# Sliding-window attention and an ELU layer on one core: the first layer's minimum made by two ScalarE activations in 56 of 144 slots, and two steps of the Strassen-Winograd tiles moved

## The chip, the cores and the metric

The kernel runs on one core of a Trainium2 chip. The core has five engines that each take their own instructions in order: TensorE (PE, with its weight loads as PEld), VectorE (DVE), ScalarE (ACT), GpSimd (POOL) and SyncE (SP), which here only issues transfers. The metric is the device time of one execution in microseconds (us), as the median of several executions. A profile of one execution goes with it.

## The reference, cut to what matters

```python
# attention: batch 8, heads 8, sequence 576, head size 64, window 128
scores = where(0 <= rel < 128, q @ k.T / 8 - slope[h] * |rel|, -1e9)
x = softmax(scores) @ v                      # reshaped to 4608 tokens x 512
# two layers, w_in 512 x 2048, w_out 2048 x 512
h = x @ w_in
g = where(h > 0, h, exp(minimum(h, 0)) - 1)  # ELU
out = g @ w_out                              # 4608 x 512, float32
```

The change touches `g` and `out`. The kernel writes the ELU as max(h, min(exp(h), 1) - 1), which is the same function; exp(minimum(h, 0)) is the same number as min(exp(h), 1).

## The kernel before, in words

The 4608 tokens are nine blocks of 512 (`NTB`). The program is written out in **slots**, numbered from 0. Each slot has at most one `hidden` step: a piece of the first layer that fills one PSUM bank with 128 x 512 numbers (two groups of 128 hidden features for 256 tokens in the later blocks, four for 128 tokens in the early ones). There are 144 such steps, one for each of slots 0 to 17 and 24 to 149. Two banks, `hp[0]` and `hp[1]`, take turns, so the `hidden` step of slot s can't start before the step of slot s-2 has been read out of its bank.

Reading out a bank takes three engines in a row. ScalarE writes e = exp(h) from the bank into SBUF (L305). GpSimd makes the minimum with 1, in place (L306). VectorE then writes g = max(e - 1, h) as float16 (`elu`, L313), reading h from the bank again, which sets the bank free. `elu` of slot s-1 is put into VectorE's queue in slot s, straight after the `hidden` step of slot s.

The main loop at the end (L646 to L659) sets the order inside a slot: the slot's early tasks (ScalarE's softmax exponentials), the `hidden` step, `elu` of the slot before, the slot's tasks (in the order in which they were registered: attention first, the sums of the second layer after that), the output matmuls, and the late tasks. As every engine takes its queue in order, that order decides who stands behind whom.

Attention for batches 2 to 7 is woven in between. A unit of 128 keys takes four slots, say from slot a: late in slot a PE makes the scores into four banks; at the head of slots a+1 and a+2 ScalarE makes two exponentials each (L231); in a+1 and a+2 VectorE multiplies them with a table (`weigh`, L236), the half for heads 0 to 3 first; in slot a+3 PE multiplies with the values (L266), heads 0 to 3 first, and VectorE divides (L271, L272). The units start at slots 32, 36, 40, 44, then 49, 53, 57, 61, then 66 and so on up to 129; after about slot 133 there is no attention left.

The second layer is done in tiles of 256 tokens, n = 0 to 17. Ten of them are plain matmuls (`output`). The eight of `SEVEN` = 5, 7, 9, 11, 13, 15, 16, 17 use the Strassen-Winograd scheme, seven block products in place of eight. For them VectorE makes four sums of blocks of g (`sums`, S1 to S4, L358 through L343) and PE makes `product` 1 to 7 with the sums and with combinations of the weights that `quarters` made beforehand in slots 41 to 48. With s = 15 + 8n, products 1, 6, 2, 7, 5, 4, 3 of tile n are spread over slots s to s+7, seven matmuls in each slot. S1 is made in slots s-2 and s-1, S2 (which reads S1) in s-1, S3 in s+1, S4 in s+3. Product 6 reads S2 and starts as the second matmul of slot s+1. The products stand in two banks, `op` and `av`, 256 columns each (`places`): 1 and 2 in one half bank, 6 and 7 in another, 5 and 3 in a third, 4 in the fourth. Product 2 adds onto product 1 in its half bank, 7 onto 6, 3 onto 5. So product 1 is copied out by ScalarE (L390, tile U1) before product 2 starts, and product 5 likewise (tile U5). VectorE's `combine` makes U2 and U3 from them and the four quarters of the result: C11 is a ScalarE copy (L392), C12, C21 and C22 are additions. C22 = U3 + U5, both in SBUF, stands among the tasks of slot s+6 (of s+8 for n = 16); C21 comes late in slot s+6, C12 late in s+7. The second half of the tile's rows is stored when both C21 and C22 are there. Tile 17, the last, has an order of its own in slots 148 to 153.

Of the kernel before, what the change touches and what calls it, by code (L numbers as in the profile page):

```python
# [10 lines left out]
AF = mybir.ActivationFunctionType  # L11
# [7 lines left out]
def kernel(  # L19
# [9 lines left out]
    nc = tc.nc  # L29
    B, H, S, D = q.shape  # L30
    NTOK, DO = out.shape
    FF = moe_w_in.shape[1]
    NFC = FF // 128
    NTB = NTOK // 512
# [114 lines left out]
    with tc.manual_schedule():  # L149
# [139 lines left out]

        es, gs, hps = {}, {}, {}  # L290

        def hidden(t, c0, w, f0, nf, p):
            hps[t, c0, f0] = p
            a = (512 * t + c0) % RING
            cuts = [(0, w, a)] if a + w <= RING else [(0, RING - a, a), (RING - a, w, 0)]
            for l in range(nf):
                fc = f0 + l
                for u0, u1, x0 in cuts:
                    for c in range(4):
                        nc.tensor.matmul(  # L300
                            p[:, l * w + u0:l * w + u1], w_in_sb[:, c, fc * 128:(fc + 1) * 128],
                            xT[:, c, x0:x0 + u1 - u0], start=(c == 0), stop=(c == 3))
            e = es[t, c0, f0] = work.tile([128, 512], F32, name="e", tag="e", bufs=6)
            n = w * nf
            nc.scalar.activation(e[:, 0:n], p[:, 0:n], AF.Exp)  # L305
            nc.gpsimd.tensor_scalar(out=e[:, 0:n], in0=e[:, 0:n], scalar1=1.0, scalar2=0.0,  # L306
                                    op0=ALU.min, op1=ALU.max)
# [30 lines left out]
        def A(n, i, k):  # L338
            c = 256 * (n % 2) + 128 * i
            return gs[n // 2][:, 8 * k:8 * k + 8, c:c + 128]  # L340

        def add(o, a, b, op=ALU.add):
            V.tensor_tensor(out=o, in0=a, in1=b, op=op)  # L343
# [6 lines left out]
        SS, U, obs = {}, {}, {}  # L350
# [9 lines left out]
        def places(n):  # L360


            x, y = (op, av) if n - 1 in SEVEN else (av, op)
            return ((x, 0), (y, 0), (x, 256), (y, 256)) if n < 2 * NTB - 1 else (
                (sp[2], 0), (sp[3], 0), (sp[0], 0), (hp[0], 0))

        def place(n, i):
            o, c = places(n)[(0, 0, 2, 3, 2, 1, 1)[i - 1]]
            return o[:, c:c + 256]

        def kept(n, i):
            if (n, i) not in U:
                U[n, i] = work.tile([128, 256], F32, name=f"U{i}", tag=f"U{i}", bufs=1)
            return U[n, i]

        def tile_out(n, i):
            if (n, i) not in obs:
                obs[n, i] = work.tile([128, DO], F32, name="ob", tag="ob")
            return obs[n, i]

        def product(n, i, j0=0, j1=8, o=None, c0=0, c1=256):
            a, b = {1: lambda: (A(n, 0, 0), WB(0, 0)), 2: lambda: (A(n, 0, 1), WB(1, 0)), 3: lambda: (SS[n, 4], WB(1, 1)),
                    4: lambda: (A(n, 1, 1), T[4]), 5: lambda: (SS[n, 1], T[1]), 6: lambda: (SS[n, 2], T[2]),
                    7: lambda: (SS[n, 3], T[3])}[i]()
            o = place(n, i) if o is None else o
            for j in range(j0, j1):
                nc.tensor.matmul(o[:, 0:c1 - c0], a[:, j, :], b[:, j, c0:c1], start=j == 0 and i in (1, 4, 5, 6),  # L387
                                 stop=j == 7, skip_group_check=True)
            if j1 == 8 and i in (1, 5):
                nc.scalar.copy(kept(n, i), o)  # L390
            if j1 == 8 and i == 2:
                nc.scalar.copy(tile_out(n, 0)[:, 0:256], o)  # L392

        def combine(n, what):
            if what == "U2":
                add(kept(n, 2), kept(n, 1), place(n, 6))
            elif what == "U3":
                add(kept(n, 3), kept(n, 1), place(n, 7))
            elif what == "C22":
                add(tile_out(n, 1)[:, 256:512], kept(n, 3), kept(n, 5))  # L400
            elif what == "C12":
                add(tile_out(n, 0)[:, 256:512], kept(n, 2), place(n, 3))
                put(n, 0, 0, DO)
            else:
                add(tile_out(n, 1)[:, 0:256], kept(n, 3), place(n, 4))
            if what in ("C22", "C21") and n < 2 * NTB - 1:
                if (n, "half") in U:
                    put(n, 1, 0, DO)
                U[n, "half"] = True

        def put(n, i, c0, c1):
            r = 256 * n + 128 * i
            nc.sync.dma_start(out[r:r + 128, c0:c1], tile_out(n, i)[:, c0:c1])

        def last_piece(n, o, c0, c1, e):
            product(n, 4, 0, 8, o, c0, c1)
            add(tile_out(n, 1)[:, c0:c1], kept(n, 3)[:, c0:c1], o[:, 0:c1 - c0])
            put(n, 1, c0, e)
# [74 lines left out]
        def at(s, f, *a):  # L493
            tasks.setdefault(s, []).append((f, a))

        def after(s, f, *a):
            late.setdefault(s, []).append((f, a))
# [14 lines left out]
        for t in range(2, NTB):  # L512
            for j in range(16):
                step = (128 * (j // 4), 128, 4 * (j % 4), 4) if t < 4 else (256 * (j // 8), 256, 2 * (j % 8), 2)
                HID[16 * t + 6 + j] = [(t, *step, BUF[(j + 1) % 2])]
        SEVEN = (17, 5, 7, 9, 11, 13, 15, 16)
        for o in range(16 * NTB):
            t, ts, f = o // 16, o // 4 % 4, o % 4
            if o // 8 in SEVEN:
                continue  # L520
            s = (9, 11, 13, 14)[o] if o < 4 else 11 + o if o < 13 else 2 * o - 1 if o < 16 else 15 + o
            OUT[s] = [(output, (t, ts, 4 * f, (op, op, sp[3], op)[ts] if t == 0 else (op, av)[ts % 2]))]

        def done(r):
            for step in HID[r]:
                elu(*step)
# [65 lines left out]
        for b in range(2, B):  # L592
# [14 lines left out]
            for n in range(4):  # L607
                piece = (b, int(n < 2), n % 2)
                if b == 2:
                    m = 4 if n < 2 else 6  # L610
# [13 lines left out]
        for n in SEVEN:  # L624
            s = 15 + 8 * n
            if n < 2 * NTB - 1:
                m = 6 if n >= 8 else 4
                for d, i, j in ((-2, 1, (0, m)), (-1, 1, (m, 8)), (-1, 2, ()), (1, 3, ()), (3, 4, ())):
                    at(s + d, sums, n, i, *j)
                at(s + (6 if n + 2 < 2 * NTB else 8), combine, n, "C22")  # L630
                for d, what in ((2, "U2"), (4, "U3"), (6, "C21"), (7, "C12")):
                    after(s + d, combine, n, what)
                for d in range(8):
                    OUT[s + d] = [(product, (n, i, j, j + 1)) for i, j in turns[7 * d:7 * d + 7]]
            else:
                at(s - 3, sums, n, 3)
                for i in (1, 2):
                    at(s - 2, sums, n, i, 0, 6)
                    at(s - 1, sums, n, i, 6, 8)
                at(s - 1, product, n, 1)  # L640
                OUT[s] = [(product, (n, 2)), (product, (n, 6)), (combine, (n, "U2")), (sums, (n, 4))]
                OUT[s + 1] = [(product, (n, 5)), (product, (n, 7)), (combine, (n, "U3"))]
                OUT[s + 2] = [(product, (n, 3)), (combine, (n, "C12")), (combine, (n, "C22")),
                              (last_piece, (n, hp[0], 128, 256, DO)), (last_piece, (n, hp[1], 0, 128, 128))]

        slots = set(HID) | set(OUT) | set(tasks) | set(early)  # L646
        for s in range(min(slots), max(slots) + 1):
            for f, a in early.get(s, []):
                f(*a)
            for step in HID.get(s, []):  # L650
                hidden(*step)
            if s - 1 in HID and s not in (1, 4, 5):
                done(s - 1)
            for f, a in tasks.get(s, []):
                f(*a)
            for f, a in OUT.get(s, []):
                f(*a)
            for f, a in late.get(s, []):
                f(*a)  # L659
# [30 lines left out]
```

## Time and profile before

| what | value |
|---|---|
| median of 8 executions | 318.13 us (317.83 to 319.32) |
| the profiled execution's own time | 317.95 us |
| its span, first to last instruction | 316.2 us |
| busy PE, PEld, DVE, ACT, POOL | 307.3, 237.7, 242.6, 178.2, 175.3 us |
| granted TensorE clock over the span | 1.000 |

The page's busy times are sums over the span; a matmul's listed end is modelled, and lies later than the moment at which the next one may start: the eight matmuls of a 256-column `hidden` step start 0.11 us apart and the step is listed with 1.03 us. Real waiting of PE is therefore read from the distance between two starts, less the work between them, and a wait that the profile lists is shorter than that by up to 0.17 us. In the lists of groups, a row gives the line, the engine, the operation, the tile written and those read, the shape, the count, and then busy us and the mean ns of one, and the idle time before them with what ended it. In the timeline a row gives the start, the duration, and then the same names, with idle time and its end in brackets.

### The profile page before, as it was taken

The page shows a single profiled execution, that of the slowest core. Times are in us where ns is not written, and L with a number is a line of the kernel's source. Part 1 is how long each engine was busy: PE and PEld are TensorE (multiplying, and loading weights), DVE is VectorE, ACT ScalarE, POOL GpSimd, SP SyncE. Part 2 cuts the span into 40 slices and gives each one's busy share as a digit, 9 for nine tenths or more (in the row PEclk, how much of TensorE's full clock was granted, in tenths as well). Part 3 has the DMA queues.
Part 4 walks back from the last instruction along what each step waited for, and adds up shares of the span by engine and source line. Part 5 has one row for each costly group of instructions (what it writes and reads, how often), then busy time and mean ns, then how long its engine had stood idle before and what let it go on. Part 6 is the DMA issues. An engine that isn't in the chain of part 4 may idle for free.

```text
span 316.2 us, 9800 instructions
## 1 busy us (share of the span) xinstructions
PE 307.3 (97%) x4119; PEld 237.7 (75%) x4119; DVE 242.6 (77%) x458; ACT 178.2 (56%) x327; POOL 175.3 (55%) x263
## 2 busy tenths in 40 slices
PE   8999999999999999999999999999999999999995
PEld 6788874887767778876887678767877787778784
DVE  5647566786689888986997798779987787576774
ACT  5575558656666466546665566556644665544330
POOL 8947878573756455664756476645623333334330
PEclk9999999999999999999999999999999999999999
DMA  9999999994979779693969699994932112120103
GB/s 100 177 198 202 202 176 162 142 122 70 100 94 111 98 84 97 76 159 62 112 69 160 98 97 64 153 127 68 75 85 55 38 21 85 52 58 2 66 2 133
DMA packets 96363, 32.02 MB, mean 101 GB/s; under 512 B 83904, under 2 KB 91840, under 8 KB 96320
## 3 DMA queue, kind: packets, MB, share of 16 engines
q0 software_dynamic: 75920, 18.36, 62.0%
q1 hardware_dynamic: 20400, 13.05, 16.5%
q8 instruction: 32, 0.52, 0.7%
q14 instruction: 11, 0.09, 0.1%
HBM read 36.70 MB, written 9.44 MB: 146 GB/s over the span
## 4 chain that ended last, share of the span: by engine, by line
PE 78%; DVE 14%; issue 3%; ACT 3%; POOL 1%; DVEq 0%; ACTq 0%
PE hp L300 32%; PE op L319 11%; PE av L319 6%; PE av L387 5%; DVE g L313 5%; PE op L387 5%; PE spa L225 4%; PE spa L266 3%; DVE S L343 2%; DVE EX L236 2%; ACT EX L231 2%; PE op L424 2%; POOL e L306 1%; DVE s L343 1%; PE sp L248 1%
## 5 line engine op out<-in xcount | busy, mean ns | idle before, releaser
L306 POOL TENSOR_SCALAR e<-e 128x512 f32<-128x512 f32 x144 | 95.8, 666 | 128.4 <-ACT e L305 127.5
L300 PE MATMUL hp<-xT,wi 128*128 128x128 f16 (+2 forms) x1744 | 144.9, 233 | 3.4 <-DVE g L313 2.9
L300 PEld LDWEIGHTS <-wi 128*128 128x128 f16 x1856 | 124.4, 98 | 31.1 <-issue 10.3
L305 ACT ACTIVATE e<-hp 128x512 f32<-128x512 f32 x138 | 82.8, 600 | 91.0 <-PE hp L300 87.3
L313 DVE SCALAR_TENSOR_TENSOR g<-e,hp 128x512 f16<-128x512 f32 x138 | 94.3, 683 | 37.8 <-POOL e L306 37.2
L319 PE MATMUL op<-wo,g 128*128 128x512 f16 x176 | 45.2, 379 | 0.0
L319 PEld LDWEIGHTS <-g 128*128 128x128 f16 x320 | 27.7, 98 | 20.5 <-issue 1.1
L236 DVE TENSOR_TENSOR EX<-EX,TAB 128x1024 f16<-128x1024 f16 x48 | 33.9, 707 | 9.7 <-ACT EX L231 9.7
L114 POOL DMA_DIRECT2D VP<-in_v_dram x40 | 34.9, 875 | 1.4 <-PE sp L319 1.0
L231 ACT ACTIVATE EX<-spa 128x512 f16<-128x512 f32 x48 | 26.1, 594 | 16.9 <-PE spa L225 16.5
L319 PE MATMUL av<-wo,g 128*128 128x512 f16 x128 | 32.8, 379 | 0.0
L387 PEld LDWEIGHTS <-S 128*128 128x128 f16 x256 | 24.5, 98 | 2.7
L231 ACT ACTIVATE EX<-sp 128x512 f16<-128x512 f32 x48 | 26.2, 606 | 0.0
L387 PEld LDWEIGHTS <-g 128*128 128x128 f16 x200 | 18.5, 98 | 2.2 <-DVE g L313 0.3
L272 DVE TENSOR_TENSOR xn<-spa,rden 128x512 f16<-128x512 f32 x24 | 16.6, 692 | 0.8
L343 DVE TENSOR_TENSOR S<-g 128x1024 f16<-128x1024 f16 (+3 forms) x24 | 16.4, 682 | 0.2
L108 POOL DMA_DIRECT2D st<-in_k_dram x24 | 16.5, 687 | 0.0
L108 POOL DMA_DIRECT2D st<-in_q_dram x24 | 16.3, 682 | 0.0
L387 PE MATMUL op<-s,S 128*128 128x256 f16 x104 | 15.6, 272 | 0.0
L225 PEld LDWEIGHTS <-KT 32*128 32x128 f16 x480 | 9.0, 92 | 8.5 <-issue 8.0
L225 PE MATMUL sp<-QT,KT 32*128 32x256 f16 (+2 forms) x240 | 15.1, 250 | 0.0
L225 PE MATMUL spa<-QT,KT 32*128 32x256 f16 (+2 forms) x240 | 15.1, 250 | 0.0
(142 smaller groups left out, 325.6 us busy)
## 6 DMA issues: line engine op xcount, KB each, us to landing
out_dram<-ob SPq DMA_DIRECT2D x35, 256.0 KB, 2.0
VP<-in_v_dram POOLq DMA_DIRECT2D x32, 128.0 KB, 4.1
st<-in_k_dram POOLq DMA_DIRECT2D x24, 144.0 KB, 3.9
st<-in_q_dram POOLq DMA_DIRECT2D x24, 144.0 KB, 3.9
wi<-in_moe_w_in_dram POOLq DMA_DIRECT2D x4, 512.0 KB, 11.4
wo<-in_moe_w_out_dram POOLq DMA_DIRECT2D x4, 512.0 KB, 11.5
VP<-in_v_dram POOLq DMA_DIRECT2D x8, 64.0 KB, 4.8
s<-in_k_dram POOLq DMA_DIRECT2D x1, 512.0 KB, 13.5
```

The costliest lines, as they stand in the source:

```text
L108: nc.gpsimd.dma_start(st[b][32 * g:32 * g + 32, w, :, :, :, :].rearrange("p h n j d -> p (h n) (j d)"), (q, k)[w][b, 2 * g:2 * g + 2, :, : ...
L114: nc.gpsimd.dma_start(VP[b % 2][0:p, n, :, 0:D], v[b, :, 128 * n:128 * n + p, :].rearrange("h p d -> p h d"))
L225: nc.tensor.matmul(sp[g][:, 256 * h2 + o:256 * h2 + o + n], kt_[b % 2][r, k0:k0 + 255:2], qt_[b % 2][r, c0:c0 + 2 * n - 1:2], start=dh == ...
L231: nc.scalar.activation(unit(b, u)[:, g, :, :], sp[g].rearrange("p (h c) -> p h c", h=2), AF.Exp, scale=0.125)
L236: V.tensor_tensor(out=e, in0=e, in1=TAB[:, int(u == 3), 2 * gp:2 * gp + 2, :, :], op=ALU.mult)
L300: nc.tensor.matmul(p[:, l * w + u0:l * w + u1], w_in_sb[:, c, fc * 128:(fc + 1) * 128], xT[:, c, x0:x0 + u1 - u0], start=(c == 0), stop=(c ...
L305: nc.scalar.activation(e[:, 0:n], p[:, 0:n], AF.Exp)
L306: nc.gpsimd.tensor_scalar(out=e[:, 0:n], in0=e[:, 0:n], scalar1=1.0, scalar2=0.0, op0=ALU.min, op1=ALU.max)
L313: V.scalar_tensor_tensor(out=gs[t][:, f0:f0 + nf, c0:c0 + w], in0=sh(es.pop((t, c0, f0))), scalar=1.0, in1=sh(hps.pop((t, c0, f0))), op0=A ...
L319: nc.tensor.matmul(o, gs[t][:, fc, ts * 128:(ts + 1) * 128], w_out_sb[:, fc, :], start=(fc == 0), stop=(fc == NFC - 1))
L343: V.tensor_tensor(out=o, in0=a, in1=b, op=op)
L387: nc.tensor.matmul(o[:, 0:c1 - c0], a[:, j, :], b[:, j, c0:c1], start=j == 0 and i in (1, 4, 5, 6), stop=j == 7, skip_group_check=True)
```

## The change

Three edits. First, `hidden` takes a flag. In the slots of a set `SOFT` the exponential and GpSimd's minimum are replaced by two ScalarE activations: relu(-h) from the bank into e, and then exp(-e) in place, which is exp(min(h, 0)). `SOFT` holds slots s-2 to s+3 of every Strassen-Winograd tile, slots 40 to 48, and all slots from 134 on. With the slots that have a `hidden` step this makes 40-48, 53-58, 69-74, 85-90, 101-106, 117-122 and 133-149: 56 of the 144. Second, S2 moves from slot s-1 to slot s. Third, C22 moves from the tasks of slot s+6 (s+8 for n = 16) to the end of slot s+5, and reads product 5 in its half bank; ScalarE's copy U5 is left out for seven of the eight tiles (tile 17 keeps it), and the store of the tile's second half follows C21.

```diff
-        def hidden(t, c0, w, f0, nf, p):
+        def hidden(t, c0, w, f0, nf, p, soft):
...
             n = w * nf
+            if soft:
+
+                nc.scalar.activation(e[:, 0:n], p[:, 0:n], AF.Relu, scale=-1.0)
+                nc.scalar.activation(e[:, 0:n], e[:, 0:n], AF.Exp, scale=-1.0)
+                return
             nc.scalar.activation(e[:, 0:n], p[:, 0:n], AF.Exp)
             nc.gpsimd.tensor_scalar(out=e[:, 0:n], in0=e[:, 0:n], scalar1=1.0, scalar2=0.0,
                                     op0=ALU.min, op1=ALU.max)
...
-            if j1 == 8 and i in (1, 5):
+            if j1 == 8 and (i == 1 or i == 5 and n == 2 * NTB - 1):
                 nc.scalar.copy(kept(n, i), o)
...
             elif what == "C22":
-                add(tile_out(n, 1)[:, 256:512], kept(n, 3), kept(n, 5))
+                add(tile_out(n, 1)[:, 256:512], kept(n, 3), kept(n, 5) if (n, 5) in U else place(n, 5))
...
             else:
                 add(tile_out(n, 1)[:, 0:256], kept(n, 3), place(n, 4))
-            if what in ("C22", "C21") and n < 2 * NTB - 1:
-                if (n, "half") in U:
-                    put(n, 1, 0, DO)
-                U[n, "half"] = True
+                put(n, 1, 0, DO)
...
-                for d, i, j in ((-2, 1, (0, m)), (-1, 1, (m, 8)), (-1, 2, ()), (1, 3, ()), (3, 4, ())):
+                for d, i, j in ((-2, 1, (0, m)), (-1, 1, (m, 8)), (0, 2, ()), (1, 3, ()), (3, 4, ())):
                     at(s + d, sums, n, i, *j)
-                at(s + (6 if n + 2 < 2 * NTB else 8), combine, n, "C22")
-                for d, what in ((2, "U2"), (4, "U3"), (6, "C21"), (7, "C12")):
+                for d, what in ((2, "U2"), (4, "U3"), (5, "C22"), (6, "C21"), (7, "C12")):
                     after(s + d, combine, n, what)
...
+        SOFT = {s for n in SEVEN for s in range(13 + 8 * n, 19 + 8 * n)} | set(range(40, 49)) | set(range(16 * NTB - 10, 16 * NTB + 8))
...
-                hidden(*step)
+                hidden(*step, s in SOFT)
```

## The prediction

> **What bounds the kernel now.** I read the page from the top (busy times, groups), then PE's waits, then the timelines of the places where PE starts late.
>
> ```profile
> PE 307.3 (97%) x4119; PEld 237.7 (75%) x4119; DVE 242.6 (77%) x458; ACT 178.2 (56%) x327; POOL 175.3 (55%) x263
> ...
> L306 POOL TENSOR_SCALAR e<-e 128x512 f32<-128x512 f32 x144 | 95.8, 666 | 128.4 <-ACT e L305 127.5
> L305 ACT ACTIVATE e<-hp 128x512 f32<-128x512 f32 x138 | 82.8, 600 | 91.0 <-PE hp L300 87.3
> L313 DVE SCALAR_TENSOR_TENSOR g<-e,hp 128x512 f16<-128x512 f32 x138 | 94.3, 683 | 37.8 <-POOL e L306 37.2
> ```
>
> PE is the bound. Only the time in which PE starts late can be won.
>
> ```profile
> PE hp L300 <- DVE g L313: 2.9, 9, 0.6
> ```
>
> Nearly all of it is this wait: a `hidden` step whose bank `elu` has not yet set free. Start to start, with 0.11 us for a 256-column matmul, the late starts from 92 us on add up to some 5.5 us: 0.7 in the quarters' slots, 3.4 from there to 260 us, 1.4 after that. So 312.5 us is a floor.
>
> The largest late start, on PE, VectorE and GpSimd:
>
> ```profile
> 294.06 0.93 PE L387 MATMUL op<-wo,g 128*128 128x256 f16 x7
> 295.54 1.03 PE L300 MATMUL hp<-xT,wi 128*128 128x256 f16 x8 [0.55 <-DVE g L313]
> ```
> ```profile
> 292.44 0.69 DVE L313 SCALAR_TENSOR_TENSOR g<-e,hp 128x512 f16<-128x512 f32 x1 [0.18 <-POOL e L306]
> 293.17 0.66 DVE L343 TENSOR_TENSOR S<-g 128x256 f16<-128x256 f16 x1
> 293.86 0.69 DVE L343 TENSOR_TENSOR S<-S,g 128x1024 f16<-128x1024 f16 x1
> 294.47 0.41 DVE L343 TENSOR_TENSOR ob<-U,av 128x256 f32<-128x256 f32 x1
> 294.80 1.47 DVE L313 SCALAR_TENSOR_TENSOR g<-e,hp 128x512 f16<-128x512 f32 x2
> ```
> ```profile
> 291.44 0.98 POOL L306 TENSOR_SCALAR e<-e 128x512 f32<-128x512 f32 x1 [1.02 <-ACT e L305]
> 293.07 0.61 POOL L306 TENSOR_SCALAR e<-e 128x512 f32<-128x512 f32 x1 [0.66 <-ACT e L305]
> ```
>
> Seven matmuls from 294.06 have had their turn at 294.83; PE goes on at 295.54, 0.71 late. Two causes stand in the rows. `elu` waits behind three additions. And where VectorE adds two SBUF operands while GpSimd makes its minimum, one of them is slow: the 128x256 sum takes 0.66 here and 0.29 alone (at 279.21), the minimum 0.98 to 1.16 in place of 0.61.
>
> **The second activation.** 56 minima leave GpSimd (56 x 0.666 = 37 us off an engine that bounds nothing); ScalarE gains 56 activations. Their price isn't in the trace: the bank-to-SBUF one is 0.600, and at 256 columns the SBUF-to-SBUF activation of the setup is 0.401 against 0.37 for a copy from a bank, so I take 0.63. Exp depends on relu just before it; nearest is VectorE's dependent pair, reciprocal 121.68 + 0.20, next start 121.92: a gap of 0.04. Bounds: -0.10 (independent activations overlap so: 1.09 for two of 0.60) and +0.3 (three times the 0.09 from ScalarE to GpSimd). The way from a `hidden` step's end to `elu` was 0.04 + 0.60 + 0.09 + 0.61 + 0.03 = 1.37 us and becomes 0.04 + 0.60 + 0.04 + 0.63 + 0.03 = 1.34 us: the same when nothing collides, 0.3 to 0.5 shorter where the minimum collided. It holds only while ScalarE is free when the bank is full.
>
> *The end, from 275.6 us on.* ScalarE is busy 12.9 of 32.3 us there, so 17 x 0.63 = 10.7 more fits. At 281.48 PE is 0.25 late because the minimum at 279.61 took 1.10; gone. At 293.19 it is 0.23 late (minimum 0.98); gone. At 295.54: S1's second part 0.29, S2 a slot later, C12 at about 293.2, so `elu` can start when exp ends, 292.36 + 0.04 + 1.27 = 293.7, not 294.80; all 0.71 gone. S2 then runs after that `elu`, with more than a slot before product 6. In the last slots the addition of 0.85 at 306.03 loses its collision and C22 of tile 16 (0.42, behind tile 17's sums) has left: 0.2 of late start at 307.87 goes. Sum 1.4 us.
>
> Unchanged there is a slack of only 0.18 per two slots (`elu` at 297.94 ends at 298.63, the bank's next step starts at 298.81). If the gap between the two activations were 0.3 rather than 0.04, PE would lose about 0.1 a slot, some 1.2 us. U1's copy now stands behind two activations: it ends about 2.6 us after its slot's start, product 2 needs it at 2.7. It fits barely; for two tiles here I take off 0.1 each: 1.2 us.
>
> *The attention stretches, slots 53 to 122.* Here ScalarE is full:
>
> ```profile
> 211.00:222.70 11.70, 11.25 (x117) 8.79 (x110) 10.85 (x18) 8.39 (x17) 6.07 (x9) 1.00 0.64 77
> 243.40:255.60 12.20, 11.85 (x134) 9.11 (x133) 9.45 (x17) 7.27 (x14) 3.42 (x6) 1.00 0.16 40
> ```
>
> (The fourth busy figure is ScalarE's.) Six more activations, start to start about 0.55 us each, are 3.3 us: 11.7 of 11.7 and 10.6 of 12.2. In slots a+1 and a+2 the two pairs of softmax exponentials (0.5 us apart) and two times 1.2 us make 4.4 us in slots of 1.65 to 1.75: a backlog of 0.7 to 1 us that slots a+3 and a+4 work off. Queued behind it are the second pair of exponentials, then `weigh` for heads 4 to 7, then (in VectorE's order) S2, and PE's values and product 6.
>
> I followed five tiles on paper with these durations. The clearest:
>
> ```profile
> 214.98 0.70 DVE L343 TENSOR_TENSOR S<-g 128x256 f16<-128x256 f16 x1
> 215.71 0.69 DVE L343 TENSOR_TENSOR S<-S,g 128x1024 f16<-128x1024 f16 x1
> 216.32 0.68 DVE L313 SCALAR_TENSOR_TENSOR g<-e,hp 128x512 f16<-128x512 f32 x1
> ```
>
> Tile 11: PE waited for this `elu` (0.61 late at 217.06). With S1b at 0.29 and S2 gone it starts at 215.75, and 0.58 is won. But S2 now follows the division (0.20 + 0.69 after that `elu`) and ends at 217.9, where product 6 would come up at 217.45: 0.5 given back. Tile 13: 0.52 won at 249.69; then the exponentials, 0.4 late, hold the values (0.27) and S2 behind them product 6 (0.4): 0.2 worse than before, and again 0.1 to 0.2 at 259.6. Tile 5: 0.6 won at 120.02 and 0.36 at 128.24, 0.25 lost to S2, 0.4 to the late minimum of slot 59: 0.2 won. Tile 7: little to win (0.2), 0.4 lost: 0.2 worse. Tile 9: 0.34 won at 188.43, 0.25 given back: 0.1 won. Quarters: ScalarE's later exponentials eat what the two sums of 1.10 (0.64 alone) give: 0.1 won. Together 0.1 won (0.2 - 0.2 + 0.1 + 0.1 - 0.2 + 0.1). I take that, nearest to the rows; the ends are 3.7 won (all 4.1 of late starts from 92 to 260 us, without the 0.4 of C22 below) and 3.3 lost (each of eleven units loses 0.3 of the 0.6 by which its second pair comes late).
>
> **C22 earlier, one copy less.**
>
> ```profile
> 228.89 0.83 DVE L343 TENSOR_TENSOR ob<-U,U 128x256 f32<-128x256 f32 x1
> 229.65 0.41 DVE L343 TENSOR_TENSOR ob<-U,op 128x256 f32<-128x256 f32 x1
> 229.98 0.67 DVE L313 SCALAR_TENSOR_TENSOR g<-e,hp 128x512 f16<-128x512 f32 x1
> ```
>
> Here C22 (two SBUF operands, colliding with a minimum outside `SOFT`) and C21 stand ahead of an `elu` for which PE waits: 0.34 late at 230.70, and in the same way 0.09 at 198.34. Late in the slot before, product 5 ends some 0.8 us before the next minimum does (226.3 and 227.1 for this tile), so a C22 of 0.41 (the row of an addition from a bank) runs in VectorE's idle time, or delays an `elu` that has 0.5 of slack. Queued behind the waiting C22 is that `elu`; behind it PE, two slots on. Won: 0.4; bounds 0 and 0.43, or 0.3 lost if product 5 is late in two tiles. The copy U5 (7 x 0.37) leaves ScalarE after the crowded slots and is worth nothing by itself. The same product 5 must be read before product 3 begins at the end of slot s+6, a slot later; covered. SP's queue: the stores keep their order; tile 16's comes two slots earlier, off the end, and the last store (313.20 + 2.0 to land) is another tile's. POOL's queue: the loads of q, k and v start up to 0.6 us earlier in 37 us less of minima; they are two batches' slots ahead and wait for nothing here.
>
> **The sum.** 1.2 + 0.1 + 0.4 = 1.7 us off the profiled execution's 317.95 (span 316.2 and 1.75 around it): 316.25. That execution lies 0.18 under the median, so I forecast 316.4.
>
> **A rule weighed.** The trace's VectorE is 77% busy, GpSimd 55%, ScalarE 56%. The Trainium skill ("ScalarE: Activation LUTs", Rules for kernel authors) advises VectorE, not ScalarE, for relu, max and min, as VectorE can be several times faster per element. By that rule the minimum would rather be a VectorE pass; with a third of 0.63 us (an estimate by that page's factor of up to three) it would add 56 x 0.2 = 12 us to the engine that `elu` waits for, and the change as made would be the worse choice. The rows say otherwise at the end (VectorE 24.2 of 32.3 us busy, ScalarE 12.9) and agree with it in slots 101 to 106.
>
> **The rivals.**
> 1. *Slower: ScalarE becomes the bound of the attention stretches.* Place: the second pair of exponentials of eleven units with a `SOFT` slot in a+1 or a+2; price 0.3 us each, half of the 0.6 that they come late, 3.3 us in all, less 1.6 won elsewhere: 319.8. It decides from 0.15 us a unit. For it: the 11.7 of 11.7. Against: values need heads 4 to 7 only 0.33 us after they begin, and most `elu` here had collisions to lose.
> 2. *The late S2 takes the place of the wait removed, and the exp gap that of the minimum.* Product 6 waits 0.4 in five tiles (2.0, of which 1.15 is in the sum: 0.85 more), or the gap is 0.3 and the end gives back 1.2: 316.4 + 0.9 to 1.3, about 317.5.
> 3. *The attention stretches win too.* ScalarE's backlog is taken up by slack and 1.7 of 3.7 comes: 314.8.
> 4. *Relu isn't in the loaded table.* One table load is 1283 ns (at 0.7 us) and there is no other although copies and exponentials alternate; 112 would be 144 us. I give it 1 in 100, outside the range.
>
> **How the numbers follow.** A measurement of this kernel tells 0.2% (0.64 us) from no change: 317.5 and 318.8 are the bounds. Chances: forecast 0.50 (315.6 to 317.2), rival 3 0.13, rival 2 0.15 (half faster, half within 0.2%), rival 1 0.21, rival 4 0.01. Faster 0.50 + 0.13 + 0.07 = 0.70, less 0.03 for the forecast's upper edge: 0.67. Same 0.08 + 0.03 = 0.11. Slower 0.22. The range leaves out the far halves of rivals 1 and 3 and rival 4, 0.18 in all: 314.8 to 319.8.
>
> **What the profile after would show.** Right: two ScalarE rows of about 0.60 and 0.63, 56 each, start to start 0.64; 88 minima; no sum over 0.75 in the soft slots; no late start at 281, 293 and 295 us; C22 at 0.41 from a bank. Rivals 1 and 2: PE waiting for VectorE's `EX` or `S` in values and product 6, ScalarE's second pair of exponentials a microsecond after its scores. Wrong altogether: a gap over 0.2 between the two activations, or late starts in every slot after 134.

## The result, and the profile after

The changed kernel takes 316.20 us (median of 11 executions, 315.59 to 317.01); the kernel before took 318.32 us in the executions measured beside it (31, 317.8 to 319.86). The ratio is 0.9931, with a 95% interval of 0.9919 to 0.9943: 0.7% faster, 2.1 us. The forecast was 316.4.

The page of the changed kernel (busy time of each engine; then groups of instructions: line, engine, operation, out<-in, shape, count, busy us, mean ns, idle time before them). The change adds five lines, so L313 is now L318, L306 is L311, and L305 is L310:

```profile
PE 306.8 (97%) x4119; PEld 238.0 (76%) x4119; DVE 236.5 (75%) x458; ACT 208.1 (66%) x376; POOL 135.5 (43%) x207
...
L311 POOL TENSOR_SCALAR e<-e 128x512 f32<-128x512 f32 x88 | 55.5, 631 | 136.7 <-ACT e L310 136.2
L310 ACT ACTIVATE e<-hp 128x512 f32<-128x512 f32 x82 | 49.1, 599 | 47.6 <-PE hp L300 44.1
L307 ACT ACTIVATE e<-hp 128x512 f32<-128x512 f32 x56 | 33.5, 598 | 19.2 <-PE hp L300 16.6
...
L308 ACT ACTIVATE e<-e 128x512 f32<-128x512 f32 x56 | 35.3, 631 | 1.8
```

GpSimd lost 56 minima, ScalarE gained 56 activations of 0.631 us from SBUF to SBUF, and VectorE became 6 us shorter though it does the same 458 instructions: its additions, and `weigh`, are no longer slowed by a minimum beside them (from slot 40 on, 16 of them took more than 0.8 us before, none does after). PE's waits in the changed kernel (engine, tile and line, waited for whom, total us, times, longest):

```profile
PE hp L300 <- DVE g L318: 0.3, 1, 0.3
...
PE av L392 <- ACT ob L331: 0.2, 1, 0.2
PE op L392 <- DVE S L348: 0.2, 1, 0.2
```

The wait of `hidden` steps for `elu` went from 2.9 us in 9 places to 0.3 in one, and that one (slot 9, where neither kernel differs) was there before. Two new ones stand in its place. The place that the prediction began with, PE and VectorE in the changed kernel:

```profile
292.62 1.04 PE L300 MATMUL hp<-xT,wi 128*128 128x256 f16 x8
293.49 0.93 PE L392 MATMUL op<-wo,g 128*128 128x256 f16 x7
294.25 1.04 PE L300 MATMUL hp<-xT,wi 128*128 128x256 f16 x8
```
```profile
292.43 0.29 DVE L348 TENSOR_TENSOR S<-g 128x256 f16<-128x256 f16 x1
292.82 0.42 DVE L348 TENSOR_TENSOR ob<-U,av 128x256 f32<-128x256 f32 x1
293.34 0.69 DVE L318 SCALAR_TENSOR_TENSOR g<-e,hp 128x512 f16<-128x512 f32 x1
293.95 0.68 DVE L348 TENSOR_TENSOR S<-S,g 128x1024 f16<-128x1024 f16 x1
```

S1's second part is back at 0.29 (from 0.66), S2 stands behind `elu`, and PE goes from slot 143 to slot 144 in 1.63 us where it took 2.35.

**Where the time went, stretch by stretch.** From slot 24 on, the distance between the first matmuls of two `hidden` steps hardly varies from one trace to another: stretches in which two kernels have the same program differ by 0.02 us at most, and from 16 us on the granted clock is 1.00 in every trace. So a stretch tells 0.05 us, though there is one trace of each kernel, where the whole execution tells half a microsecond. The table gives the difference to the kernel before, in us (minus is faster). The last row of sums runs from the `hidden` step of slot 24 to PE's last matmul, 257.08 us before and 254.26 after. The four columns on the right are the first four experiments below.

| slots | predicted | the change | activations alone | moves alone | activations at the end only | in attention only |
|---|---|---|---|---|---|---|
| 39-49, quarters | -0.1 | -0.21 | -0.21 | 0.00 | -0.01 | -0.21 |
| 53-63, tile 5 | -0.2 | -0.59 | -0.67 | -0.14 | -0.15 | -0.60 |
| 69-80, tile 7 | +0.2 | 0.00 | -0.04 | +0.17 | +0.17 | 0.00 |
| 85-92, tile 9 | -0.1 | -0.19 | -0.18 | 0.00 | 0.00 | -0.19 |
| 92-96, its C22 | -0.09 | -0.08 | +0.02 | -0.08 | -0.08 | -0.08 |
| 101-108, tile 11 | -0.1 | -0.21 | -0.20 | -0.25 | -0.25 | -0.22 |
| 108-112, its C22 | -0.34 | -0.34 | -0.15 | -0.34 | -0.34 | -0.34 |
| 117-128, tile 13 | +0.2 | -0.02 | -0.14 | +0.19 | +0.19 | -0.02 |
| 133-137, tile 15 | -0.25 | 0.00 | 0.00 | -0.24 | 0.00 | -0.24 |
| 137-149, tiles 15, 16 | -0.74 | -0.98 | -0.72 | -0.69 | -0.98 | -0.70 |
| 149 to PE's end | -0.2 | -0.20 | -0.20 | -0.06 | -0.20 | -0.06 |
| slot 24 to PE's end | -1.7 | -2.82 | -2.48 | -1.42 | -1.64 | -2.63 |

The two profiled spans are only 0.9 us apart (316.2 and 315.2), because of what lies outside these stretches. In the execution after, the first `hidden` step began at 13.77 us, before at 12.62, though both kernels run the same program up to there; slots 0 to 24 took 0.16 us longer, and the time from PE's last matmul to the end 0.56 us. Whether the medians' 2.1 us fall short of the traces' 2.8 us for the same reasons isn't shown, as one execution of each kernel was traced; more on that in the last section.

### The profile page after: what moved, and what is told of

The parts are those of the page before. It is cut to its first block, busy times and chain, and to the rows that moved or that the text cites. A ratio compares the mean times of both kernels' runs of the same rounds, so it can differ in the third digit from the quotient of the medians.

```text
span 315.2 us, 9840 instructions
## 1 busy us (share of the span) xinstructions
PE 306.8 (97%) x4119; PEld 238.0 (76%) x4119; DVE 236.5 (75%) x458; ACT 208.1 (66%) x376; POOL 135.5 (43%) x207
## 4 chain that ended last, share of the span: by engine, by line
PE 88%; DVE 4%; ACT 2%; DMA 2%; issue 2%; POOL 1%; ACTq 0%; POOLq 0%; DVEq 0%
PE hp L300 37%; PE op L324 12%; PE av L324 8%; PE av L392 7%; PE op L392 6%; PE spa L225 4%; PE spa L266 3%; DMA s<-in_q_dram 2%; DVE g L318 1%; PE sp L248 1%; PE sp L324 1%; PE sp L300 1%; PE sp L392 1%; ACT EX L231 1%; PE spa L176 1%
## 5 line engine op out<-in xcount | busy, mean ns | idle before, releaser
L318 DVE SCALAR_TENSOR_TENSOR g<-e,hp 128x512 f16<-128x512 f32 x138 | 94.4, 684 | 35.2 <-POOL e L311 26.1
L311 POOL TENSOR_SCALAR e<-e 128x512 f32<-128x512 f32 x88 | 55.5, 631 | 136.7 <-ACT e L310 136.2
L310 ACT ACTIVATE e<-hp 128x512 f32<-128x512 f32 x82 | 49.1, 599 | 47.6 <-PE hp L300 44.1
L236 DVE TENSOR_TENSOR EX<-EX,TAB 128x1024 f16<-128x1024 f16 x48 | 33.1, 690 | 14.8 <-ACT EX L231 14.8
L308 ACT ACTIVATE e<-e 128x512 f32<-128x512 f32 x56 | 35.3, 631 | 1.8
```

The source lines that it names most:

```text
L236: V.tensor_tensor(out=e, in0=e, in1=TAB[:, int(u == 3), 2 * gp:2 * gp + 2, :, :], op=ALU.mult)
L308: nc.scalar.activation(e[:, 0:n], e[:, 0:n], AF.Exp, scale=-1.0)
L318: V.scalar_tensor_tensor(out=gs[t][:, f0:f0 + nf, c0:c0 + w], in0=sh(es.pop((t, c0, f0))), scalar=1.0, in1=sh(hps.pop((t, c0, f0))), op0=A ...
```

## The experiments

### The activations alone, the moves alone

```diff
-                for d, i, j in ((-2, 1, (0, m)), (-1, 1, (m, 8)), (0, 2, ()), (1, 3, ()), (3, 4, ())):
+                for d, i, j in ((-2, 1, (0, m)), (-1, 1, (m, 8)), (-1, 2, ()), (1, 3, ()), (3, 4, ())):
```

That is the first, the activations alone, and with it C22, the copy U5 and the store go back to the lines of the kernel before. The second, the moves alone:

```diff
-        SOFT = {s for n in SEVEN for s in range(13 + 8 * n, 19 + 8 * n)} | set(range(40, 49)) | set(range(16 * NTB - 10, 16 * NTB + 8))
+        SOFT = set()
```

> The two activations alone: S2 stays in slot s-1, C22 and the copy U5 stay as before. Theory A (the colliding minimum is the main cause): no sum over 0.75 us in the soft slots, most of the 2.1 us is here, 1.4 to 1.9 us faster than the kernel before; the late start of slot 144 falls from 0.7 to under 0.2. Theory B (the order in VectorE's queue is the main cause): S2 still stands ahead of elu in slot s, at most 0.7 us faster, and slot 144 stays 0.3 or more late. Both: the late start of slot 111 (0.34, C22 ahead of an elu) stays.

> S2 a slot later and C22 earlier, the minimum on GpSimd everywhere. Theory A: 0.4 to 0.8 us faster, of which 0.34 is slot 111 and about 0.36 is slot 144 (an S2 of 0.69 out of the way of one elu); minima of about 1.0 us still stand beside the sums. Theory B: 1.4 us faster or more.

Measured against the kernel before: the activations alone 315.88 us, ratio 0.9927 (0.9913 to 0.9941); the moves alone 317.34 us, ratio 0.9962 (0.9944 to 0.9979). By traces 2.48 and 1.42 us of the change's 2.82. The two edits do much of the same work. In slots 141 to 145 the change wins 0.94; the activations alone win 0.68 there and the moves alone 0.88. With the activations alone, VectorE and PE there:

```profile
291.43 0.29 DVE L348 TENSOR_TENSOR S<-g 128x256 f16<-128x256 f16 x1
291.76 0.69 DVE L348 TENSOR_TENSOR S<-S,g 128x1024 f16<-128x1024 f16 x1
292.37 0.41 DVE L348 TENSOR_TENSOR ob<-U,av 128x256 f32<-128x256 f32 x1
292.70 0.68 DVE L318 SCALAR_TENSOR_TENSOR g<-e,hp 128x512 f16<-128x512 f32 x1
```
```profile
292.40 0.93 PE L392 MATMUL op<-wo,g 128*128 128x256 f16 x7
293.43 1.03 PE L300 MATMUL hp<-xT,wi 128*128 128x256 f16 x8
```

The sums are short, S2 still stands ahead of `elu`, and PE is 0.26 late (seven matmuls from 292.40 end their turn at 293.17). Neither theory's numbers came as a pair. A put the activations alone at 1.4 to 1.9 us and the moves alone at 0.4 to 0.8; they won 2.48 and 1.42. B's 1.4 for the moves was met, but it put the activations alone at 0.7 at most. Each edit does much of the other's work, which neither theory allowed for. Over the whole kernel the activations, which end the collisions, win more (A's order); at this place the moves alone win more (B's 0.3 for the late start was close). Slot 111 was not as expected: with the activations alone 0.15 of its 0.34 went, although C22 stands where it stood.

Is it the collision that the activations take away? GpSimd also issues the loads of q, k and v, and a minimum that stands behind such an issue would be late as well. In the kernel before that was rare: of the 16 minima ahead of the late `hidden` steps from slot 44 on, 15 began 0.08 to 0.10 us after the end of their exponential, and one (slot 72) 0.24 us after it. And where nothing collides the two activations win little: 54 more of them, in a kernel below, win 0.17 us.

The moves alone make tiles 7 and 13 slower by 0.17 and 0.19 us. PE's waits there show why: S2, a slot later, is late for product 6, by 0.47, 0.36, 0.35 and 0.69 us (start to start) in tiles 5, 7, 11 and 13.

```profile
PE op L392 <- DVE S L348: 1.2, 4, 0.5
PE hp L300 <- DVE g L318: 0.9, 4, 0.3
```

### The activations at the end only, and in the attention stretches only

The first added line is that of the kernel with the activations at the end only, the second that of the other.

```diff
-        SOFT = {s for n in SEVEN for s in range(13 + 8 * n, 19 + 8 * n)} | set(range(40, 49)) | set(range(16 * NTB - 10, 16 * NTB + 8))
+        SOFT = set(range(16 * NTB - 11, 16 * NTB + 8))
...
+        SOFT = {s for n in SEVEN for s in range(13 + 8 * n, 19 + 8 * n) if s < 16 * NTB - 11} | set(range(40, 49))
```

> All three edits, but the two activations only in slots 133 to 149 (17 of the 56). Theory of the prediction (the attention stretches balance to about nothing): as fast as with all 56, within 0.3 us, so about 2 us faster than before. Theory C (the attention stretches win more than ScalarE's crowding costs, as the stretches of the trace after suggest): about 0.9 to 1.0 us from slots 141 to 145, 0.2 from the tail, 0.34 from slot 111 and a little of S2's move: 1.4 us faster than before, 0.7 slower than all 56.

> All three edits, but the two activations only in the 39 slots up to 122. Theory of the prediction: 0.5 us faster than before (0.1 from these slots, 0.4 from C22), plus about 0.4 from S2's move at the end. Theory C: about 1.2 us from slots 39 to 112, plus 0.4 at the end from the moves alone: 1.6 us faster than before.

Measured: end only 317.15 us, ratio 0.9961 (0.9946 to 0.9976); attention only 316.32 us, ratio 0.9936 (0.9920 to 0.9951). Theory C holds, with more than it said: by traces the activations in the attention stretches are worth 1.18 us (2.82 less 1.64; it said 0.7), and the 17 at the end only 0.19 (2.82 less 2.63), once the moves are in. The prediction had it the other way round. With S2 and C22 moved, nearly all that was late at the end is gone without the activations, and in slots 133 to 137 they even cost 0.24.

### What the 0.24 in slot 135 is

ScalarE and PE in the changed kernel:

```profile
278.61 0.60 ACT L307 ACTIVATE e<-hp 128x512 f32<-128x512 f32 x1 [0.96 <-PE hp L300]
279.24 0.63 ACT L308 ACTIVATE e<-e 128x512 f32<-128x512 f32 x1
279.77 0.57 ACT L331 COPY ob<-av 128x512 f32<-128x512 f32 x1
```
```profile
279.27 1.04 PE L300 MATMUL hp<-xT,wi 128*128 128x256 f16 x8
280.39 0.92 PE L392 MATMUL av<-wo,g 128*128 128x256 f16 x7
```

The copy of the last plain tile (`store`, out of bank `av`) stands in ScalarE's queue behind both activations of slot 134 and ends at 280.34. Product 1 of tile 15 writes `av` and starts at 280.39, 0.25 after the `hidden` step before it has had its turn. The same wait stands before product 1 of tiles 5, 11 and 13 (0.23, 0.38 and 0.25 us late). Tiles 7 and 9 follow a plain tile too; there the copy ends in time. Two ways to take it out: let tiles 5 to 15 begin in the other bank, or take slots 133 and 134 out of `SOFT`.

```diff
-            x, y = (op, av) if n - 1 in SEVEN else (av, op)
+            x, y = (av, op) if n == 16 else (op, av)
```

> The change with the two banks of tiles 5 to 15 exchanged, so that product 1 goes into the bank that the last plain tile did not use. Theory D (product 1 waits for ScalarE's copy of that tile, which now stands behind two activations): the late starts before product 1 of tiles 5, 11, 13 and 15 (0.23, 0.38, 0.25 and 0.25) go; where nothing takes their place 1.1 us faster than the change, at least 0.5. Rival: elu is as late as the copy and PE waits at the next hidden step instead: no gain. A new wait may come eight slots later, where the next plain tile begins in the bank that C12 reads last; at most 0.2 for each tile.

Measured: 315.83 us, ratio 0.9902 (0.9879 to 0.9924). By the trace 0.26 us faster than the change, not 1.1. Tile 15 wins its 0.24, tile 11 0.06, tiles 5 and 13 nothing. The waits of the four copies are gone. In tiles 5 and 11 another takes the place: product 6 waits 0.24 and 0.33 us for S2, where it waited 0.07 and nothing in the change. In tile 13 product 6 waited 0.32 us in the change already and waits 0.35 now; what comes in there is 0.20 us of PE between the two halves of the values, which are ready for heads 4 to 7 only when `weigh` is done. Tile 11 with the banks exchanged, PE and VectorE:

```profile
215.39 0.93 PE L392 MATMUL op<-wo,g 128*128 128x256 f16 x7
216.15 1.04 PE L300 MATMUL hp<-xT,wi 128*128 128x256 f16 x8
217.02 0.27 PE L392 MATMUL op<-wo,g 128*128 128x256 f16 x1
217.46 0.83 PE L392 MATMUL av<-s,S 128*128 128x256 f16 x6 [0.16 <-DVE S L348]
```
```profile
215.27 0.69 DVE L318 SCALAR_TENSOR_TENSOR g<-e,hp 128x512 f16<-128x512 f32 x1 [0.25 <-ACT e L308]
215.88 0.20 DVE L271 RECIPROCAL rden<-spa 128x8 f32<-128x8 f32 x1
216.11 0.69 DVE L272 TENSOR_TENSOR xn<-spa,rden 128x512 f16<-128x512 f32 x1
216.72 0.68 DVE L348 TENSOR_TENSOR S<-S,g 128x1024 f16<-128x1024 f16 x1
```

Product 1 starts at once, product 6 would follow at 217.13, S2 ends at 217.40. In the change itself S2's lateness in this tile, and most of it in tile 5, was hidden behind the copy's. Which of the rival's forms it would be was expected wrongly too: not `elu`, but S2.

### S2 back in slot s-1, for all tiles and for three

```diff
-                for d, i, j in ((-2, 1, (0, m)), (-1, 1, (m, 8)), (0, 2, ()), (1, 3, ()), (3, 4, ())):
+                for d, i, j in ((-2, 1, (0, m)), (-1, 1, (m, 8)), (-1, 2, ()), (1, 3, ()), (3, 4, ())):
...
+                for d, i, j in ((-2, 1, (0, m)), (-1, 1, (m, 8)), (-1 if n in (5, 7, 13) else 0, 2, ()), (1, 3, ()), (3, 4, ())):
...
+        SOFT -= {133, 134}
```

The first added line is for all tiles; the other two, together, are the mixture.

> The change with S2 back in slot s-1. If S2's lateness makes product 6 wait behind the attention's sums, tiles 5, 7 and 13 win 0.08, 0.04 and 0.12 us as in the run with the activations alone, and slots 141 to 145 lose 0.26 there; C22's move stays worth 0.1 and 0.2 to 0.35. Sum: within 0.2 us of the change. The prediction's price (0.4 lost to S2 in three tiles) would make it 0.8 us faster than the change.

> S2 early for tiles 5, 7 and 13 alone, and slots 133 and 134 without the second activation, so that the copy of the last plain tile (ScalarE, after slot 134's activations) doesn't hold tile 15's first product. Stretch by stretch the best of the runs so far: 0.25 us at slot 135 and 0.24 in the three tiles, 0.5 us faster than the change; 2.6 to 2.8 us faster than the kernel before. If the stretches don't add, no faster than the change.

Measured: all tiles 315.99 us, ratio 0.9932 (0.9919 to 0.9945); the mixture 316.32 us, ratio 0.9939 (0.9926 to 0.9951). By traces the first is 0.08 us faster than the change: tiles 5, 7 and 13 win 0.09, 0.04 and 0.13, slots 141 to 145 lose 0.17. That is the small price and not the prediction's. It also means that once the two activations are in, moving S2 for all tiles gains nothing; what it wins at the end it loses in the three tiles. The mixture is 0.50 us faster from slot 24 to PE's end, as the stretches added up, 0.24 of it in slots 133 to 137. Its median doesn't show it: the execution's start and end vary by more.

### ScalarE's load doubled

```diff
+        SOFT = set(range(40, 16 * NTB + 8))
```

> The two activations in all 110 slots from 40 to 149: the suspected cost, ScalarE's crowding, doubled. There is nothing to win in the added slots (their minima collide with little and PE starts in time there). Rival 1 of the prediction (half of the 0.6 us by which the second pair of exponentials comes late reaches PE): eleven more units at 0.3 us, about 3 us slower than the change with 56. Theory C (PE's slack takes the backlog up): within 0.7 us of it.

Measured: 315.82 us, ratio 0.9933 (0.9911 to 0.9956); by the trace 0.17 us faster than the change. ScalarE is busy 239.5 of 314.1 us there, and in a 12 us window over tile 11 (start and end; span, then busy time and count of PE, PEld, DVE, ACT and POOL):

```profile
211.00:223.00 12.00, 11.78 (x116) 9.34 (x115) 10.16 (x19) 11.09 (x22) 0.00 (x0) 1.00 0.37 53
```

ScalarE at 92% of a stretch costs PE no more there than in the change (in both, product 1 of tile 11 waits 0.38 us for the copy). Rival 1 falls: eleven more crowded units brought no 3 us; one stretch (49 to 53) lost 0.17, four others won 0.35 together.

### The minimum on VectorE

In the 56 slots ScalarE makes one activation, and `elu` begins with the minimum, in place, on VectorE.

```diff
-                nc.scalar.activation(e[:, 0:n], p[:, 0:n], AF.Relu, scale=-1.0)
-                nc.scalar.activation(e[:, 0:n], e[:, 0:n], AF.Exp, scale=-1.0)
+                nc.scalar.activation(e[:, 0:n], p[:, 0:n], AF.Exp)
...
+                V.tensor_scalar(out=e[:, 0:w * nf], in0=e[:, 0:w * nf], scalar1=1.0, scalar2=0.0,
+                                op0=ALU.min, op1=ALU.max)
```

> In the 56 slots VectorE makes the minimum, in place and just before elu, and ScalarE has one activation; S2 and C22 as in the change. The skill's rule (relu, max, min belong on VectorE): not slower than the change. My estimate: VectorE is the engine that elu queues on; 0.3 to 0.6 us more per slot (a third of an activation up to the 0.42 of a 256-column addition and more) where it is 92% busy (slots 101 to 106) lets most of it reach PE: 4 to 15 us slower than the change, and even at the end (24.2 + 17 x 0.45 = 32 of 32.3 us) slower.

Measured: 325.45 us, ratio 1.0227 (1.0213 to 1.0241) where the change has 0.9931; by the trace 9.92 us slower than the change. The group of the minima, and PE's wait:

```profile
L319 DVE TENSOR_SCALAR e<-e 128x512 f32<-128x512 f32 x56 | 24.7, 440 | 0.3 <-ACT e L307 0.3
```
```profile
PE hp L300 <- DVE g L322: 5.8, 15, 0.6
```

Each stretch with a tile in attention loses 0.6 to 1.4 us, the quarters 2.8. In slots 101 to 108, where the prediction took the rows to side with a VectorE pass, it is 1.36. The pass itself is shorter than ScalarE's (0.42 against 0.63 us), as the Trainium skill's rule has it ("ScalarE: Activation LUTs", Rules for kernel authors: relu, max and min on VectorE), but by a factor of 1.5 in float32, where the page gives up to about 3 in bf16. What decides is the queue. VectorE sat idle before these 56 minima for 0.3 us in all; ahead of 52 of them the exponential had ended 0.1 to 2.5 us earlier. The pass stood behind VectorE's additions, and then held `elu`, for which PE waits, by its own length. Together the 56 took 24.7 us, twice the 12 us that the prediction estimated for such passes, and PE ended 9.9 us later.

### C22 where it was

```diff
-                for d, what in ((2, "U2"), (4, "U3"), (5, "C22"), (6, "C21"), (7, "C12")):
+                at(s + (6 if n + 2 < 2 * NTB else 8), combine, n, "C22")
+                for d, what in ((2, "U2"), (4, "U3"), (6, "C21"), (7, "C12")):
```

(The copy U5 is back, too.)

> The change with C22 and the copy U5 back as before (in slot s+6, from SBUF). If C22's place is what 0.4 us of the change come from, slots 108 to 112 are 0.15 to 0.35 us slower than with the change and slots 92 to 96 are 0.1 slower; if the minimum's collision in slot 109 was the cause, which stays on GpSimd in both, no difference of place shows. The rest unchanged: 0.3 us slower than the change in all.

Measured: 316.41 us, ratio 0.9915 (0.9892 to 0.9938); by the trace 0.31 us slower than the change, 0.10 in slots 92 to 96 and 0.19 in 108 to 112, nothing elsewhere. VectorE and GpSimd in the latter stretch, first with C22 late:

```profile
229.03 0.42 DVE L348 TENSOR_TENSOR ob<-U,U 128x256 f32<-128x256 f32 x1
229.37 0.41 DVE L348 TENSOR_TENSOR ob<-U,op 128x256 f32<-128x256 f32 x1
229.96 0.69 DVE L318 SCALAR_TENSOR_TENSOR g<-e,hp 128x512 f16<-128x512 f32 x1 [0.17 <-POOL e L311]
```
```profile
229.04 0.89 POOL L311 TENSOR_SCALAR e<-e 128x512 f32<-128x512 f32 x1 [1.69 <-ACT e L310]
```

and then in the change, where C22 has been made one `elu` earlier, from its bank (0.38 at 227.13):

```profile
228.93 0.41 DVE L348 TENSOR_TENSOR ob<-U,op 128x256 f32<-128x256 f32 x1
229.58 0.69 DVE L318 SCALAR_TENSOR_TENSOR g<-e,hp 128x512 f16<-128x512 f32 x1 [0.23 <-POOL e L311]
```
```profile
228.93 0.61 POOL L311 TENSOR_SCALAR e<-e 128x512 f32<-128x512 f32 x1 [1.69 <-ACT e L310]
```

C22 from two SBUF operands still collides with a minimum. In the kernel before VectorE paid (0.83 for C22), here GpSimd does (0.89 for the minimum), and `elu` waits for it: 0.28 us later than in the change with the 0.1 by which the two traces stand apart there taken off. An addition that reads one operand from a bank doesn't collide. In whole executions the difference can't be told from nothing.

### The best of the stretches together

Banks exchanged, S2 early for tiles 5, 7 and 13, and then also the two activations in slot s+4.

```diff
+            x, y = (av, op) if n == 16 else (op, av)
...
+                for d, i, j in ((-2, 1, (0, m)), (-1, 1, (m, 8)), (-1 if n in (5, 7, 13) else 0, 2, ()), (1, 3, ()), (3, 4, ())):
...
+        SOFT = {s for n in SEVEN for s in range(13 + 8 * n, 20 + 8 * n)} | set(range(40, 49)) | set(range(16 * NTB - 10, 16 * NTB + 8))
```

The last line is in the second kernel only.

> The same with S2 in slot s-1 for tiles 5, 7 and 13. If the two add, another 0.25 us: 1.3 faster than the change, 3.4 faster than the kernel before. Where product 1 no longer waits, product 6 comes earlier and S2's place weighs more: up to 0.5 faster than the run without it.

> The same again, with the two activations also in slot s+4 of each tile (five more slots), since the late starts in slots s+6 (0.08 to 0.23) follow a minimum of slot s+4 that begins late behind ScalarE's backlog: 0.3 us faster than the run without it if that is so, no difference if the backlog itself sets it.

Measured: 316.13 us, ratio 0.9915 (0.9892 to 0.9938), and 315.19 us, ratio 0.9889 (0.9869 to 0.9909). From slot 24 to PE's end 253.70 and 253.56 us, against the change's 254.26: 0.55 and 0.70 faster, and 0.15 between the two rather than 0.3. By traces the first is 0.29 us faster than the banks exchanged alone (0.25 said); its median isn't. Slot s+4 gave 0.05 in tile 5 and 0.11 in tile 13. The last kernel is the fastest of all, by the trace and by its ratio. The kernel before took 318.92 us beside these runs and 318.32 beside the change, so only ratios compare: 0.9889 against 0.9931 is 1.3 us, more than the trace's 0.70, and what the rest is isn't shown.

## Why the prediction was right, point by point

The time and the sign were right, and so was the mechanism of the first edit: the collisions go, and with them nearly all of PE's waits for `elu`. Of the three terms of the sum one was far off and one was right by two errors that cancel; that the forecast lies so near is in part luck.

- **The second activation's price.** Right. Exp from SBUF takes 0.631 us (0.63 said), and follows relu after 0.03 us (0.04 said; relu starts at 278.61 with 0.60, exp at 279.24).
- **The end, 1.2 us.** Measured 1.18, with two errors that cancel. "At 281.48 PE is 0.25 late because the minimum took 1.10; gone" failed: the minimum went, and the store's copy, one activation later in ScalarE's queue, held product 1 for 0.25 us. The prediction asked what stands behind the second activation and named U1's copy only; the 0.2 taken off for that was not lost. And the 0.71 at 295.54 was put down to the sum's collision and to S2's place together; either alone would have done most of it (0.68 and 0.88 of the 0.94 in slots 141 to 145). In the last slots the activations alone win all of the 0.20.
- **The attention stretches, 0.1 won.** Mis-sized: 1.22 us. Tile 5 won 0.59 instead of 0.2: the late minimum of slot 59 cost 0.08 where 0.4 was said (and the tile's own terms, 0.6 + 0.36 - 0.25 - 0.4, make 0.3). Tile 13 lost nothing instead of 0.2: a late start of 0.34 us at 257.51, which the text on this tile leaves out, went too; the 0.1 to 0.2 at 259.6, named there but not in its -0.2, did come (0.23). Tile 7 lost 0.23 of late starts and not 0.4, tiles 9 and 11 and the quarters won 0.1 more each. S2's lateness, priced at 0.25, 0.5 and 0.4 us in tiles 5, 11 and 13, was seen as 0.07, none and 0.32. In tiles 5 and 11 that price was not wrong in kind: the exchange of banks shows 0.24 and 0.33 there. PE was already held by the copy that the prediction overlooked (0.23 and 0.38), and of two waits that overlap only the part by which the later one ends last is paid.
- **C22, 0.4 us.** Right: 0.08 and 0.34, and the moves alone win all of it. The activations alone win 0.15 of the 0.34, so that with them in, C22's place is worth 0.10 and 0.19.
- **Rivals.** ScalarE's crowding (1) is ruled out by the path that it names, the second exponentials: with 54 more activations the kernel isn't slower. Crowding did cost by another path, the copy ahead of product 1. S2 in place of the wait (2) is a true mechanism, worth 0.2 to 0.35 a tile, and partly hidden; its price was 0.85 beyond the sum because it counts three tiles (1.15), while the sum has 0.4 and 0.25 lost in tiles 7 and 9 as well. The attention stretches that win too (3) is what the traces show, with 1.2 where it said 1.7: rival 3 is nearer to what happened than the account behind the forecast. Relu needed no table load (4): its rows are 578 to 610 ns, and the trace has the one load at the start and no other.
- **The sum.** By the traces the terms make 2.8 us, not 1.7; the median moved by 2.1. Had the median followed the traces, the time would have been some 315.5. That the forecast of 316.4 lies so near to 316.2 is luck to that extent: the gain in the attention stretches was put 1.1 us too low, and something outside the stretches took 0.7 us in the executions measured. What that was isn't settled; in the profiled execution a later start, slots 0 to 24 and a later end took 1.9 us.

## What to carry to other kernels

When an instruction is added to an engine's queue, list everything behind it, its copies out of PSUM above all, and ask which matmul writes those banks next: PE waits for the bank, not for the result. An engine at 90% of a stretch need not be a bound if what queues on it has slack, while a shorter pass just ahead of the instruction that frees the next bank can reach PE: here 24.7 us of such passes cost 9.9. Where several small waits stand at one place, remove them together and compare stretches between fixed points of the traces: single edits overlap, and a wait that is hidden by another shows only when that one is gone.

## What the runs showed of the hardware

- The first `hidden` step began at 12.35 to 15.01 us in fourteen profiles with the same instructions up to there. In the five latest (13.36 us and up) PE waits 0.9 to 1.7 us for the load of q in the setup. PE in the kernel with the moves alone:

```profile
8.54 0.63 PE L136 MATMUL hp<-ident,s 64*64 64x64 f16 x16 [1.68 <-DMA s<-in_q_dram]
```

- From PE's last matmul to the end of the span it was 3.5 us in eight profiles and 4.0 to 4.5 in six, with the same three last stores at the same distances. The last of them landed 2.4 us after that matmul in the eight and 2.8 to 3.2 us in the six; why isn't shown. All six are kernels with the activations in the last slots and C22 early, but so are two of the eight, so whether the change itself lengthens the end stays open. In the profiles these two spreads are the largest; slots 0 to 24 took 42.7 to 43.2 us, and from there on like stretches agree to 0.02 us.
- An addition of two SBUF operands beside GpSimd's minimum made one of the two 0.3 to 0.6 us longer, VectorE's or GpSimd's (0.83 for C22 in place of 0.42 in the kernel before; 0.89 for the minimum in place of 0.61 in the kernel with C22 late); ScalarE's activations from SBUF to SBUF beside the same additions stayed between 629 and 637 ns.
